# Second MLP's third token tile by seven block products of 256 columns, some collects by accumulating DMA, and weight rings divided by part

## The chip, the core and the metric

The kernel runs on one NeuronCore of a Trainium2 chip. Five engines run their own instruction streams beside each other: TensorE (PE in the profile) multiplies matrices, VectorE (DVE), ScalarE (ACT) and GpSimd (POOL) work on elements, SyncE (SP) issues DMAs. They wait for one another by semaphores. The metric is the time of one execution on the device in microseconds (us), the median of several.

## The reference

Attention with decay over blocks of 64 positions gives x, 1,536 tokens by 512. Two MLPs follow:

```python
x = np.ascontiguousarray(attn_out.transpose(0, 2, 1, 3)).reshape(B * S, H * D)   # 1536 x 512
h = x @ w_in                      # first MLP, 512 x 2048
g = h * np.clip(h + 3.0, 0.0, 6.0) / 6.0
x = g @ w_out                     # 2048 x 512
h = x @ w_in                      # second MLP, other weights
g = np.maximum(0.01 * h, h)
out = g @ w_out
```

The weights come as 64-bit numbers and are turned into fp32 in the kernel. Every fp32 operand of an MLP is split into a high and a low part (names ending in `h` and `l`), and a product is three matmuls: high x high, high x low, low x high.

## The kernel before, in words

The tokens are three tiles `t` of 512 columns, the 2,048 hidden units 16 slices `f` of 128. For a slice, `gemm1` makes the hidden 128 x 512 values of a tile: four chunks of the 512 inputs by three matmuls, 12 matmuls. A gate on ScalarE and VectorE makes `Gh` and `Gl` of them, and `gemm2` adds the slice's part to four banks `acc0` to `acc3` in PSUM, three matmuls each. Slices go in blocks (`BLOCKS`): after a block's last slice `collect` moves the four banks of a tile away and adds them to the tile's sums in SBUF (`SUM[t]`); ScalarE copies them in a first block, VectorE adds them in later ones, and in the first MLP's last two blocks banks 0 and 2 are instead filled with the sums before the block begins (`seeded`).

Tiles 0 and 1 (`PAIR`) are not multiplied so from the first MLP's fourth block on: two slices and two tiles form a 2 x 2 block product, made with seven products of 6 matmuls instead of eight (`pair`, `product`). S1 to S4 are sums of weight blocks, T1 to T4 sums of x blocks, `keep` copies a partial result and `join` adds two. The third tile goes on with `gemm1` (`one`).

The order on every engine comes from a planner, `Order`: operations are added with an engine, a planned cost, what they follow, which buffers they take and free, and a due time; `issue` plays the plan and writes the instructions in the order in which they start there. The due times of the paired blocks come from the list `line`. A weight half goes through `load_w` (DMA on SP into a `raw` buffer), `low_bits`, `magnitude`, `exponent`, `compose`, then `w_high` (ScalarE) and `w_low` (VectorE). Before, a slice's two halves, w_in (`j = 0`) and w_out (`j = 1`), lie in one buffer of the ring `w`, taken and freed together.

Of the kernel before, what the change touches and what calls it, by code (L numbers as in the profile page):

```python
# [20 lines left out]
DM = H * D  # L21
# [95 lines left out]
def decay_attention_two_mlps(ctx: ExitStack, tc: tile.TileContext, qkk, vv, lam, w1, w2, out):  # L117
# [3 lines left out]
    sizes = {"raw": 4, "cv": 3, "cl": 2, "w": 6, "G": 3, "u": 3, "h": 2, "a": 2, "r": 3, "vs": 3}  # L121
# [246 lines left out]
    cut = lambda l, f, j, hl: W[l, f][hl][:, j, :]  # L368
# [38 lines left out]
    def w_high(h):  # L407
        def fn(_):
            l, f, j = h
            if j == 0:  # L410
                W[l, f] = [new("w", [P, 2, DM], F32R, n) for n in ("wh", "wl")]
            nc.scalar.copy(out=cut(*h, 0), in_=CV[h][0].bitcast(F32))  # L412
        return fn

    def w_low(h):
        return lambda e: eng[e].tensor_tensor(out=cut(*h, 1), in0=CV[h][0].bitcast(F32), in1=cut(*h, 0).bitcast(F32),  # L416
                                              op=ALU.subtract)
# [24 lines left out]
    alloc_w, composed, low = {}, {}, {}  # L442
    for l in range(2):
        for f in range(NF):
            for j in range(2):
# [8 lines left out]
                hi = add(("act", 0.62), w_high(h), after=[c, alloc_w.get((l, f))], takes=[] if j else ["w"])  # L454
                alloc_w[l, f] = hi
# [10 lines left out]
    PH, U, G, ACC = {}, {}, {}, {}  # L466

    def gemm1(s):
        def fn(_):
            l, b, t, f = steps[s]  # L470
            xh, xl = X[t]
            wh, wl = W[l, f]
            ps = PH[s] = new("a" if paired(l, f) else "h", [P, TT], F32)
            n = 0
            for k in range(KC):
                ws = slice(k * P, (k + 1) * P)
                for a, x in ((wh, xh), (wh, xl), (wl, xh)):
                    nc.tensor.matmul(ps, a[:, 0, ws], x[:, k, :], start=(n == 0), stop=(n == 3 * KC - 1))  # L478
                    n += 1
# [34 lines left out]
    seeded = lambda s, e: steps[s][0] == 0 and steps[s][1] >= SINGLE and e % 2 == 0  # L514
# [8 lines left out]
    def gemm2(s, e):  # L523
        def fn(_):
            l, b, t, f = steps[s]
            wh, wl = W[l, f]
# [8 lines left out]
            if l == 0:  # L535
                terms = ((wh[:, 1, es], gh), (wh[:, 1, es], gl), (wl[:, 1, es], gh))
            else:
                terms = ((gh[:, es], wh[:, 1]), (gh[:, es], wl[:, 1]), (gl[:, es], wh[:, 1]))
# [3 lines left out]
            PA["acc", s, e] = ACC[e]  # L542
        return fn

    def collect(s, e):
        def fn(x):
            l, b, t, f = steps[s]
            ps, acc = PA["acc", s, e], SUM[t][:, e, :]
            if b and not seeded(s, e):
# [3 lines left out]
        return fn  # L553

    def split_x(t, e, lo):
        def fn(_):
            xh, xl = (x[:, e:e + 2] for x in X[t])
            if lo:
                nc.vector.tensor_tensor(out=xl, in0=SUM[t][:, e:e + 2], in1=xh.bitcast(F32), op=ALU.subtract)
            else:  # L560
                nc.scalar.copy(out=xh, in_=SUM[t][:, e:e + 2])
        return fn
# [11 lines left out]
    PAIR = (0, 1)  # L574
    XT, CS, SPARE = {}, {}, {}
    A_B = (("A11", "B11"), ("S1", "T1"), ("A12", "B21"), ("S2", "T2"), ("S4", "B22"), ("S3", "T3"), ("A22", "T4"))
    BANK = (0, 2, 1, 0, 2, 0, 0)

    def open_late(_):
# [4 lines left out]
        for n in ("T1", "T2", "T4"):  # L584
            XT[n] = [xt.tile([P, 2, TT], F32R, name=f"{n}{i}") for i in "hl"]
        (XT["B11"], XT["B21"]), (XT["T3"], XT["B22"]) = (
            [[x[:, e:e + 2] for x in X[t]] for e in (0, 2)] for t in PAIR)

    def whole(n):
        t, e = {"B11": (0, 0), "T1": (0, 0), "B21": (0, 2), "T4": (0, 2),  # L590
                "B12": (1, 0), "T3": (1, 0), "B22": (1, 2), "T2": (1, 2)}[n]
        return SUM[PAIR[t]][:, e:e + 2]

    def x_sum(n, a, b):
        return lambda _: nc.vector.tensor_tensor(out=whole(n), in0=whole(a), in1=whole(b), op=ALU.subtract)

    def x_split(n, lo, src=whole):
        def fn(e):
            xh, xl = XT[n]
            if lo:  # L600
                eng[e].tensor_tensor(out=xl, in0=src(n), in1=xh.bitcast(F32), op=ALU.subtract)
            else:
                nc.scalar.copy(out=xh, in_=src(n))
        return fn


    def spare(n):
        i = {"B11": 0, "T1": 0, "B12": 1, "T3": 1, "B22": 2, "T2": 2, "B21": 3, "T4": 3}[n]
        return SPARE[i // 2][:, i % 2]

    def x_whole(n):
        t, e = {"B11": (0, 0), "B21": (0, 2), "B12": (1, 0), "B22": (1, 2)}[n]

        def fn(g):
            if n in ("B11", "B22"):
                SPARE[n == "B22"] = pool["s"].tile([P, 2, 2, TT], F32, tag="s", name="x_spare")
            xh, xl = (x[:, e:e + 2].bitcast(F32) for x in X[PAIR[t]])
            eng[g].tensor_tensor(out=spare(n), in0=xh, in1=xl, op=ALU.add)
        return fn

    def x_diff(n, a, b):
        return lambda e: eng[e].tensor_tensor(out=spare(n), in0=spare(a), in1=spare(b), op=ALU.subtract)

    def product(l, p, i):
        def fn(_):
            an, bn = A_B[i]
            if i < 2:
                PA["S", l, p, BANK[i]] = new("h", [P, TT], F32)
            ps, xs = PA["S", l, p, BANK[i]], XT[bn]
            if an[0] == "S":  # L630
                ws = [SB[l, p][:, hl, int(an[1]) - 1] for hl in range(2)]
# [253 lines left out]
```

## Time and profile before

| what | value |
|---|---|
| median of 3 runs (567.62 to 570.68) | 568.48 us |
| the profiled execution's own time | 570.67 us |
| its span, first to last instruction | 568.5 us |
| busy share PE, DVE, ACT, POOL | 98%, 76%, 58%, 5% |
| mean granted clock of TensorE | 0.991 |

An engine's busy share says how long it had an instruction, not that it was the limit: what an engine waited for, and the chain of work that ended last, tell that.

### The profile page before, as it was taken

What the parts mean: (1) busy time and instruction counts of PE and PEld (TensorE: products, weight loads), DVE (VectorE), ACT (ScalarE), POOL (GpSimd) and SP (SyncE); (2) the same over time, 40 slices, a digit from 0 to 9 for tenths busy, and PEclk for the clock granted to TensorE, in tenths of its full rate; (3) what the DMA queues carried; (4) which work ended last, traced back from release to release, by engine and by line L of the source; (5) the groups of instructions that cost most, each with busy time, mean ns of one, the idle gap of its engine ahead of it and who ended that gap; (6) DMA issues with size and microseconds to landing.
All of it is one profiled execution on the core that took longest, in us unless ns stands there. A gap on an engine that the chain in (4) does not pass through costs nothing.

```text
span 568.5 us, 8504 instructions
## 1 busy us (share of the span) xinstructions
PE 554.9 (98%) x3372; PEld 460.3 (81%) x3372; DVE 430.0 (76%) x696; ACT 329.1 (58%) x554; POOL 28.2 (5%) x33
## 2 busy tenths in 40 slices
PE   8879999999999999999999999999999999999996
PEld 5778888888888888888888888888888888888885
DVE  8668999998998988789798896778754988552222
ACT  5677885555355775488575885687336744343110
POOL 6543000000000000000000000000000000000000
PEclk9798999999999999999999999999999999999999
DMA  8884233331023202221220222422211121000332
GB/s 336 313 320 148 81 108 108 112 112 39 0 75 110 76 37 75 79 107 37 76 74 1 74 75 74 149 74 75 79 70 37 39 77 35 0 1 0 75 74 74
DMA packets 14536, 49.81 MB, mean 88 GB/s; under 512 B 1698, under 2 KB 1698, under 8 KB 14498
## 3 DMA queue, kind: packets, MB, share of 16 engines
q1 hardware_dynamic: 14176, 48.77, 25.6%
q8 instruction: 26, 0.43, 0.3%
q10 hardware_dynamic: 322, 0.52, 0.3%
q14 instruction: 12, 0.10, 0.1%
HBM read 46.14 MB, written 3.15 MB: 87 GB/s over the span
## 4 chain that ended last, share of the span: by engine, by line
PE 96%; issue 1%; DMA 1%; POOL 1%; DVE 0%; SPq 0%; POOLq 0%
PE acc L540 44%; PE h L638 17%; PE h L478 12%; PE a L478 11%; PE a L638 3%; PE pair L274 2%; PE a L299 2%; PE h L311 2%; PE a L540 2%; DMA vs<-vv 1%; DVE sums L550 0%; POOL kd L264 0%; PE h L179 0%; POOL vs L260 0%; SPq L243 0%
## 5 line engine op out<-in xcount | busy, mean ns | idle before, releaser
L550 DVE TENSOR_TENSOR sums<-acc,sums 128x512 f32<-128x512 f32 x68 | 45.6, 688 | 24.8 <-PE acc L540 24.8
L507 DVE TENSOR_TENSOR Gl<-u,Gh 128x512 fp32r<-128x512 f32 x32 | 22.1, 689 | 45.2 <-ACT Gh L658 45.2
L540 PE MATMUL acc<-Gh,wh 128*128 128x512 f32 x144 | 56.1, 390 | 0.0
L540 PE MATMUL acc<-Gh,wl 128*128 128x512 f32 x144 | 56.0, 389 | 0.0
L540 PE MATMUL acc<-Gl,wh 128*128 128x512 f32 x144 | 56.0, 389 | 0.0
L540 PE MATMUL acc<-wh,Gh 128*128 128x512 f32 x128 | 49.8, 389 | 0.0
L540 PE MATMUL acc<-wl,Gh 128*128 128x512 f32 x128 | 49.8, 389 | 0.0
L540 PE MATMUL acc<-wh,Gl 128*128 128x512 f32 x128 | 49.8, 389 | 0.0
L664 ACT ACTIVATE u<-a 128x512 f32<-128x512 f32 x24 | 14.4, 599 | 59.4 <-PE a L478 57.6
L416 DVE TENSOR_TENSOR wl<-t,wh 128x512 fp32r<-128x512 f32 x64 | 43.0, 686 | 7.4 <-ACT wh L412 7.3
L404 DVE CUSTOM_DVE_ANT_0 t<-t,c 128x1024 uint16<-128x1024 uint16 x64 | 45.2, 706 | 2.2
L412 ACT CAST wh<-t 128x512 fp32r<-128x512 f32 x64 | 39.1, 617 | 13.0 <-DVE t L404 12.1
L381 ACT ACTIVATE c<-raw 128x512 uint32<-128x512 uint32 x64 | 42.8, 671 | 4.8 <-DVE t L404 3.6
L385 ACT ACTIVATE t<-raw 128x512 f32<-128x512 f32 x64 | 42.7, 666 | 4.6 <-DVE wl L416 4.6
L402 DVE SCALAR_TENSOR_TENSOR t<-raw,t 128x512 uint32<-128x512 uint32 x64 | 44.1, 689 | 1.3
L487 ACT ACTIVATE u<-h,three 128x512 f32<-128x512 f32 x28 | 19.3, 689 | 40.6 <-PE h L478 36.9
L478 PE MATMUL h<-xh,wh 128*128 128x512 f32 x96 | 37.6, 391 | 0.0
L478 PE MATMUL h<-xh,wl 128*128 128x512 f32 x96 | 37.4, 389 | 0.0
L478 PE MATMUL h<-xl,wh 128*128 128x512 f32 x96 | 37.4, 389 | 0.0
L478 PE MATMUL a<-xh,wh 128*128 128x512 f32 x96 | 37.3, 389 | 0.0
L478 PE MATMUL a<-xl,wh 128*128 128x512 f32 x96 | 37.3, 389 | 0.0
L478 PE MATMUL a<-xh,wl 128*128 128x512 f32 x96 | 37.3, 389 | 0.0
(149 smaller groups left out, 1315.9 us busy)
## 6 DMA issues: line engine op xcount, KB each, us to landing
raw<-w SPq DMA_DIRECT2D x64, 512.0 KB, 3.3
sums<-qkk SPq DMA_DIRECT2D x12, 768.0 KB, 7.2
vs<-vv SPq DMA_DIRECT2D x6, 512.0 KB, 7.1
out<-sums SPq DMA_DIRECT2D x20, 128.0 KB, 2.4
out<-sums ACTq DMA_DIRECT2D x4, 128.0 KB, 3.2
lam_sb<-lam ACTq DMA_DIRECT2D x1, 0.0 KB
```

Of the source, the lines that this page charges most:

```text
L381: nc.scalar.activation(out=CV[h][1], in_=RAW[h][:, :, 0], func=AF.Copy, scale=2.0 ** -29)
L385: return lambda _: nc.scalar.activation(out=CV[h][0].bitcast(F32), in_=RAW[h][:, :, 1].bitcast(F32), func=AF.Abs)
L402: nc.vector.scalar_tensor_tensor(out=t, in0=RAW[h][:, :, 1], scalar=0xC0000000, in1=t, op0=ALU.bitwise_and, op1=ALU.bitwise_or)
L404: nc.vector.tensor_tensor(out=t, in0=t, in1=c, op=ALU.add)
L412: nc.scalar.copy(out=cut(*h, 0), in_=CV[h][0].bitcast(F32))
L416: return lambda e: eng[e].tensor_tensor(out=cut(*h, 1), in0=CV[h][0].bitcast(F32), in1=cut(*h, 0).bitcast(F32), op=ALU.subtract)
L478: nc.tensor.matmul(ps, a[:, 0, ws], x[:, k, :], start=(n == 0), stop=(n == 3 * KC - 1))
L487: nc.scalar.activation(out=U[s], in_=at_src(s), func=AF.Relu, bias=three, scale=1.0)
L507: nc.vector.tensor_tensor(out=gl, in0=U[s], in1=gh.bitcast(F32), op=ALU.subtract)
L540: nc.tensor.matmul(ACC[e], a, x, start=(first and n == 0 and not seeded(s, e)), stop=(last and n == 2), skip_group_check=seeded(s, e))
L550: nc.vector.tensor_tensor(out=acc, in0=ps, in1=acc, op=ALU.add)
L638: nc.tensor.matmul(ps, ws[a][:, k * P:(k + 1) * P], xs[b][:, k], start=(i < 2 and n == 0), stop=(n == 5), skip_group_check=True)
```

## The change

The third tile of the second MLP is cut into two halves of 256 columns, and they are multiplied with two slices by the same seven products, each of 256 columns (`half_pair`, `product_1`, `keep_1`, `join_1`); `gemm1` stays for the first MLP. The seven products are put into another order. In every block but a first and a last one of each MLP, banks 0 to 2 are collected in another way: ScalarE copies the bank into a buffer of the new ring `st`, and GpSimd issues a DMA that adds it to the sums in SBUF (`by_dma`, `add_up`). In the first MLP's last block all four banks are seeded, and the second tile's sums of that block are read from PSUM directly (`sums_pair`, `late_x`). The sums of x blocks for the first MLP are begun by DMAs (`x_whole`) where VectorE made them. The ring `w` becomes `w0` and `w1`, each of half slices, and `raw` has 3 buffers where it had 4.

The diff, cut to its core:

```diff
-    sizes = {"raw": 4, "cv": 3, "cl": 2, "w": 6, "G": 3, "u": 3, "h": 2, "a": 2, "r": 3, "vs": 3}
+    sizes = {"raw": 3, "cv": 3, "cl": 2, "w0": 4, "w1": 5, "st": 2, "G": 3, "u": 3, "h": 2, "a": 2, "r": 3, "vs": 3}
...
-            l, f, j = h
-            if j == 0:
-                W[l, f] = [new("w", [P, 2, DM], F32R, n) for n in ("wh", "wl")]
-            nc.scalar.copy(out=cut(*h, 0), in_=CV[h][0].bitcast(F32))
+            W[h] = [new(f"w{h[2]}", [P, DM], F32R, n) for n in ("wh", "wl")]
+            nc.scalar.copy(out=W[h][0][:, cols(*h)], in_=CV[h][0].bitcast(F32)[:, cols(*h)])
...
-                hi = add(("act", 0.62), w_high(h), after=[c, alloc_w.get((l, f))], takes=[] if j else ["w"])
-                alloc_w[l, f] = hi
+                hi = add(("act", 0.62), w_high(h), after=[c], takes=[f"w{j}"])
...
-    seeded = lambda s, e: steps[s][0] == 0 and steps[s][1] >= SINGLE and e % 2 == 0
+    seeded = lambda s, e: steps[s][0] == 0 and steps[s][1] == len(BLOCKS[0]) - 1
+    by_dma = lambda s, e: e < 3 and 0 < steps[s][1] < len(BLOCKS[steps[s][0]]) - 1
+    kept = lambda s, e: seeded(s, e) and steps[s][2] == PAIR[1]
+    STAGE, ACC_AT = {}, {}
+
+    def add_up(s, e):
+        t = steps[s][2]
+        return lambda _: nc.gpsimd.dma_start(out=SUM[t][:, e, :], in_=STAGE[t, e], accum_op=ALU.add)
...
+            if by_dma(s, e):
+                STAGE[t, e] = new("st", [P, TT], F32)
+                nc.scalar.copy(out=STAGE[t, e], in_=ps)
+            elif b and not seeded(s, e):
                 nc.vector.tensor_tensor(out=acc, in0=ps, in1=acc, op=ALU.add)
...
-    A_B = (("A11", "B11"), ("S1", "T1"), ("A12", "B21"), ("S2", "T2"), ("S4", "B22"), ("S3", "T3"), ("A22", "T4"))
-    BANK = (0, 2, 1, 0, 2, 0, 0)
+    A_B = (("A11", "B11"), ("S1", "T1"), ("S2", "T2"), ("A12", "B21"), ("S3", "T3"), ("S4", "B22"), ("A22", "T4"))
+    BANK = (0, 2, 0, 1, 0, 2, 0)
...
+    def x_whole(k, n, lo):
+        def fn(_):
+            if not lo and (n == "B11" or n == "B22" and not k):
+                SPARE[k, int(n == "B22")] = pool["s"].tile([P, 2 << k, 2, TT >> k], F32, tag="s", name=f"x_spare{k}")
+            x = part([x[lo].bitcast(F32) for x in X], k, n)
+            if lo:
+                nc.gpsimd.dma_start(out=spare(k, n), in_=x, accum_op=ALU.add)
+            else:
+                nc.sync.dma_start(out=spare(k, n), in_=x)
+        return fn
...
+    def product_1(l, p, i):
+        def fn(_):
+            if i == 0:
+                PA["X", l, p] = new("a", [P, TT], F32)
+            terms(l, p, i, 1, PA["XY"[i in (2, 4, 6)], l, p][:, hi_cols if i in (1, 5) else lo_cols], i == 0)
+        return fn
+
+    def keep_1(l, p, i):
+        def fn(_):
+            x = PA["X", l, p]
+            if i:
+                CS[l, p, "5"] = new("ux", [P, TT], F32)
+                nc.scalar.copy(out=CS[l, p, "5"][:, lo_cols], in_=x[:, hi_cols])
             else:
-                k = 2 * P * (int(an[2]) - 1)
-                ws = [w[:, 0, k:k + 2 * P] for w in W[l, 2 * p + int(an[1]) - 1]]
-            n = 0
-            for k in range(2):
-                for a, b in ((0, 0), (0, 1), (1, 0)):
-                    nc.tensor.matmul(ps, ws[a][:, k * P:(k + 1) * P], xs[b][:, k], start=(i < 2 and n == 0),
-                                     stop=(n == 5), skip_group_check=True)
-                    n += 1
-        return fn
+                PA["Y", l, p] = new("a", [P, TT], F32)
+                nc.scalar.copy(out=PA["Y", l, p][:, lo_cols], in_=x[:, lo_cols])
+        return fn
+
+    def join_1(l, p, n):
+        return lambda _: nc.vector.tensor_tensor(out=PA[n, l, p][:, hi_cols], in0=PA["Y", l, p][:, lo_cols],
+                                                 in1=CS[l, p, "5"][:, lo_cols], op=ALU.add)
...
+            far = by_dma(s, e)
+            c = add(("dve", 0.69) if b and not in_seed and not far else ("act", 0.58), collect(s, e),
+                    due2[s] + T_COLLECT, after=[prev2, *([] if far else taken.get((t, e), []))], frees=[bank],
+                    takes=["st"] * far)
+            bank_last[bank] = c
+            if far:
+                c = add(("pool", 1.2), add_up(s, e), due2[s] + T_COLLECT, after=[c, *taken.get((t, e), [])])
+                c = add(("dma2", 2.5), nothing, due2[s] + T_COLLECT, after=[c], frees=["st"])
...
+        if l:
+            line = [*(two(0, i) for i in range(4)), one(0), *(two(1, i) for i in range(4)), one(2), two(2, 0), two(2, 1)]
...
+    def half_pair(l, p, after_a):
+        f1, f2 = 2 * p, 2 * p + 1
+        d, at = due_p["1", l, f1], 0
+        ops = []
+
+        def prod(i, after=(), takes=()):
+            nonlocal at
+            an, bn = A_B[i]
+            w = s_ready[l, p] if an[0] == "S" else w_ready[l, 2 * p + int(an[1]) - 1, 0]
+            ops.append(add(("pe", 0.72), product_1(l, p, i), d + at, after=[w, *x_op[l, 1, bn], *ops[-1:], *after],
+                           takes=list(takes)))
+            last_s[l, 1, bn] = ops[-1]
+            at += 0.72
+            return ops[-1]
+
+        k1 = add(("act", 0.42), keep_1(l, p, 0), after=[prod(0, after_a, takes=["a", "a"])])
+        k5 = add(("act", 0.42), keep_1(l, p, 1), after=[prod(1)], takes=["ux"])
+        v = add(("dve", 0.42), join_1(l, p, "X"), after=[prod(2, [k1]), k5])
+        p2 = prod(3)
+        c22 = add(("dve", 0.42), join_1(l, p, "Y"), after=[prod(4, [v])], frees=["ux"])
+        p3 = prod(5, [v])
+        p4 = prod(6, [c22])
+        for f, n, after in ((f1, "X", [p2, p3]), (f2, "Y", [p4, c22])):
+            s = at_step[l, 2, f]
+            add_ps = add(("none", 0.0), lambda _, s=s, n=n: PH.__setitem__(s, PA[n, l, p]), after=after)
+            gates(s, [add_ps], "a")
+        half_at[0] = ops[0]
+        return ops
...
+        ops = [pair(l, f // 2) for f in fs[::2]]
+        for f, o in zip(fs[::2], ops):
+            if l:
+                add(("none", 0.0), nothing, after=o + half_pair(l, f // 2, ops[1][3:4]), frees=["s", "w0", "w0"])
```

How the built programs stand. TensorE, second MLP, third block, third tile: before, the hidden values of one slice (`x` 105 and 106 are the tile's high and low part, `a` the PSUM bank), first rows of 12 with the group ahead:

```order
L540 MATMUL acc_4403<-wl,Gh 128x512
L540 MATMUL acc_4403<-wh,Gl 128x512
L478 MATMUL a<-xh_105,wh 128x512
L478 MATMUL a<-xl_106,wh 128x512
L478 MATMUL a<-xh_105,wl 128x512
```

And after, second block, third to fifth product of a pair of slices (T21 is T2 for the half tiles, `s` a sum of weight blocks, `acc` 4298 and 4323 banks 0 and 1, in brackets the engines whose semaphores are waited for):

```order
L546 MATMUL acc_4298<-wh,Gl 128x512 [waits DVE_49]
L636 MATMUL a<-T21h,s 128x256 [waits Activation_49]
L636 MATMUL a<-T21l,s 128x256
L636 MATMUL a<-T21h,s 128x256 x2
L636 MATMUL a<-T21l,s 128x256
L636 MATMUL a<-T21h,s 128x256
L636 MATMUL a<-xh_111,wh 128x256 [waits Activation_49]
L636 MATMUL a<-xl_112,wh 128x256
L546 MATMUL acc_4323<-wh,Gh 128x512
L636 MATMUL a<-xh_111,s 128x256 [waits DVE_49]
```

What moved: two slices' 24 matmuls of 512 columns stood in two closed pieces that waited for nothing of their own; now 42 of 256 columns stand between groups of `gemm2`, and the third, fourth, fifth and seventh product wait for copies and joins of earlier ones.

ScalarE after, at the end of the second block's first tile of the second MLP (`acc0` to `acc2` are its banks; `a` and `ux` the half products' PSUM bank and buffer):

```order
L557 COPY st_4118<-acc0_4000 128x512 [waits PE_49]
L557 COPY st_4125<-acc1_4016 128x512 [waits PE_49]
L664 COPY a_4148<-a_4137 128x256 [waits PE_49]
L557 COPY st_4156<-acc2_4024 128x512 [waits DMASW7_49,Activation_49]
L661 COPY ux_4164<-a_4137 128x256 [waits PE_49]
L686 ACTIVATE Gxh_4182<-ux_4004 128x512 [waits DVE_49,PE_49]
```

At the same place before, the collects stood on VectorE:

```order
L550 TENSOR_TENSOR sums_100<-acc0_3886,sums_100 128x512 [waits PE_49]
L550 TENSOR_TENSOR sums_100<-acc1_3906,sums_100 128x512 [waits PE_49]
L550 TENSOR_TENSOR sums_100<-acc2_3912,sums_100 128x512 [waits PE_49]
L550 TENSOR_TENSOR sums_100<-acc3_3920,sums_100 128x512 [waits PE_49]
```

What moved: three of four collects went from VectorE to ScalarE, and the copy of bank 2 has a wait for a DMA that GpSimd issued, with the copy of the second half product (`ux`) behind it.

## Rows read from the trace of the kernel before

**Rows 1.** The page: span, busy time of each engine, granted clock in 40 slices.

```profile
span 568.5 us, 8504 instructions
PE 554.9 (98%) x3372; PEld 460.3 (81%) x3372; DVE 430.0 (76%) x696; ACT 329.1 (58%) x554; POOL 28.2 (5%) x33
...
PEclk9798999999999999999999999999999999999999
```

**Rows 2.** The waits of PE: us in total, times, longest.

```profile
PE pair L274 <- issue: 5.5, 2, 3.2
PE a L299 <- POOL kd L264: 1.1, 1, 1.1
PE h L179 <- DVE zeros L184: 1.1, 1, 1.1
PE a L299 <- issue: 0.7, 1, 0.7
PE h L311 <- POOL vs L260: 0.2, 1, 0.2
```

**Rows 3.** The chain that ended last: start us, us, what.

```profile
37.79 3.20 issue
...
472.32 2.72 PE a L478 x12
...
548.48 5.44 PE acc L540 x24
556.64 4.77 PE acc L540 x21
561.43 2.73 DVE sums L550 x4
```

**Rows 4.** Busy us by stretch; after POOL come granted clock, DMA share, GB/s.

```profile
312.00:370.00 58.00, 58.00 (x257) 47.86 (x257) 45.82 (x79) 42.53 (x73) 0.00 (x0) 1.00 0.27 91
...
430.00:490.00 60.00, 60.00 (x266) 49.71 (x265) 46.15 (x78) 32.05 (x55) 0.00 (x0) 1.00 0.14 45
```

**Rows 5.** Timeline of matmuls (PE) and weight loads (PEld): start us, us.

```profile
400.30 0.39 PE L540 MATMUL acc<-wl,Gh 128*128 128x512 f32 x1
400.31 0.19 PEld L540 LDWEIGHTS acc<-wh,Gl 128*128 128x128 f32 x1
400.53 0.39 PE L540 MATMUL acc<-wh,Gl 128*128 128x512 f32 x1
```

**Rows 6.** Weight loads by form: count, busy us, mean ns, idle before.

```profile
L478 PEld LDWEIGHTS a<-xh,wh 128*128 128x128 f32 x96 | 18.0, 188 | 3.8
...
L274 PEld LDWEIGHTS pair<-sums 64*64 64x64 f32 x384 | 13.7, 145 | 7.3 <-issue 5.7 <-DMA sums<-qkk 0.4 <-ACT vs L304 0.4
L179 PEld LDWEIGHTS <-zeros 128*128 128x128 bf16 x18 | 1.7, 115 | 3.2 <-issue 1.4 <-DVE zeros L184 1.1
```

**Rows 7.** Timeline of PE in the warm-up and the attention.

```profile
12.32 1.04 PE L179 MATMUL h<-zeros 128*128 128x512 bf16 x4
...
31.20 1.15 PE L274 MATMUL pair<-sums 64*64 64x64 f32 x32
32.27 1.15 PE L299 MATMUL a<-vs,kd 128*64 128x64 f32 x32
```

**Rows 8.** Groups on ACT and DVE: count, busy us, mean ns, idle before.

```profile
L552 ACT COPY sums<-acc 128x512 f32<-128x512 f32 x34 | 19.8, 589 | 4.3 <-PE acc L540 2.8
L664 ACT ACTIVATE u<-a 128x512 f32<-128x512 f32 x24 | 14.4, 599 | 59.4 <-PE a L478 57.6 <-PE a L638 1.8
L213 ACT COPY u<-h 128x252 f32<-128x252 f32 x1 | 0.4, 369 | 0.9 <-PE h L208 0.9
...
L550 DVE TENSOR_TENSOR sums<-acc,sums 128x512 f32<-128x512 f32 x68 | 45.6, 688 | 24.8 <-PE acc L540 24.8
L507 DVE TENSOR_TENSOR Gl<-u,Gh 128x512 fp32r<-128x512 f32 x32 | 22.1, 689 | 45.2 <-ACT Gh L658 45.2
L428 DVE TENSOR_TENSOR raw<-t 128x256 f32<-128x256 f32 x24 | 10.1, 420 | 0.2
L404 DVE CUSTOM_DVE_ANT_0 t<-t,c 128x1024 uint16<-128x1024 uint16 x64 | 45.2, 706 | 2.2
```

**Rows 9.** DMA issues (KB each, median us to landing), and POOL's longest group.

```profile
raw<-w SPq DMA_DIRECT2D x64, 512.0 KB, 3.3
sums<-qkk SPq DMA_DIRECT2D x12, 768.0 KB, 7.2
...
out<-sums SPq DMA_DIRECT2D x20, 128.0 KB, 2.4
...
L264 POOL TENSOR_TENSOR kd<-sums,decay 64x512 f32<-64x512 f32 x22 | 25.2, 1145 | 18.4 <-issue 9.3 <-PE a L299 5.8 <-POOL kd L264 2.4
```

More of the change, by code (lines that the diff above doesn't have):

```diff
@@ L594, in x_sum @@
[L594 to L599, printed above, removed]
+        for k in range(2):
+            for n in ("T1", "T2", "T4"):
+                XT[k, n] = [xt.tile([P, 2, TT >> k], F32R, name=f"{n}{k}{i}") for i in "hl"]
+            for n in ("B11", "B21", "T3", "B22"):
+                XT[k, n] = [part([x[i] for x in X], k, n) for i in range(2)]
@@ L604, in x_split @@
         return fn
[L607 to L618, printed above, removed]
-        return fn
@@ new lines, in terms @@
+    def terms(l, p, i, k, ps, first):
+        an, bn = A_B[i]
+        xs = XT[k, bn]
+        if an[0] == "S":
+            ws = [SB[l, p][:, hl, int(an[1]) - 1] for hl in range(2)]
+        else:
+            c = 2 * P * (int(an[2]) - 1)
+            ws = [w[:, c:c + 2 * P] for w in W[l, 2 * p + int(an[1]) - 1, 0]]
+        n = 0
+        for c in range(2):
+            for a, b in ((0, 0), (0, 1), (1, 0)):
+                nc.tensor.matmul(ps, ws[a][:, c * P:(c + 1) * P], xs[b][:, c], start=(first and n == 0),
+                                 stop=(n == 5), skip_group_check=True)
+                n += 1
@@ L685, in second @@
                 continue
-            c = add(("dve", 0.69) if b and not in_seed else ("act", 0.58), collect(s, e), due2[s] + T_COLLECT,
-                    after=[prev2, *taken.get((t, e), [])], frees=[bank])
+            if kept(s, e):
+                sums.append(prev2)
+                continue
+            far = by_dma(s, e)
[6 more added lines that the diff above has]
+                c = add(("dma2", 2.5), nothing, due2[s] + T_COLLECT, after=[c], frees=["st"])
             sums.append(c)
-            bank_last[bank] = c
             taken[t, e] = [c]
@@ L708, in decay_attention_two_mlps @@
             due_p[item] = at
-            at += 9.52 if item[0] == "S" else 2.72
-        rest = [] if end else [two(2, 2), two(2, 3)]
+            at += {"S": 9.52, "1": 5.04 if l else 2.72, "2": 2.72}[item[0]]
+        rest = [two(2, i) for i in range(3 if end else 2, 4)]
     for item in rest:
@@ L772, in pair @@
             gate[s] = add(("dve", 0.69), g_low(s), after=[gh], frees=[free]), n
-        add(("none", 0.0), nothing, after=ops, frees=["s"])
+        return ops
     def seconds(l, b):
@@ L785, in decay_attention_two_mlps @@
             if steps[s][1] == b:
[L786 removed]
+                g = one(s, x_of(steps[s][2]))
+                calm = g if steps[s][2:] == (1, starts[0][2] - 1) else calm
         seconds(0, b)
     op_late = add(("none", 0.0), open_late, after=att_ops, frees=[n for n in late for _ in range(late[n])])
[L792 to L796 removed]
```

245 lines of the change are left out of this document (143 added, 102 removed).

## The prediction

> **What bounds the kernel now.** The first view is the page's busy table: TensorE (PE) is busy for 98% of the span of 568.5 us, VectorE for 76%, ScalarE for 58% [rows 1]. A share alone proves nothing, so the second view is what TensorE waited for: five rows, 8.6 us in all, and every one of them belongs to the attention or the warm-up at the start [rows 2]. After the attention TensorE waits for nobody. The third view is the chain that ended last: its last pieces are TensorE, TensorE, TensorE and then four collects on VectorE, 561.43 to 564.16 us, with the store behind them [rows 3]. In the second MLP the stretches say the same: TensorE is busy for all of 312 to 370 us and of 430 to 490 us, at granted clock 1.00, which is its level of 2.4 GHz, while VectorE is busy for 45.8 of 58.0 us and 46.2 of 60.0 us, and ScalarE for 42.5 and 32.1 us [rows 4]. So from some 70 us on time is saved only by fewer TensorE microseconds, and lost by anything that makes TensorE wait. Relief for VectorE is worth nothing by itself.
>
> **TensorE's work.** Before, the third token tile of the second MLP takes 12 matmuls of 512 columns for each slice f, 16 slices, 192 matmuls. The chain has twelve of them as one piece of 2.72 us [rows 3], so one takes 2.72/12 = 0.2267 us (the 0.39 us of one record is with its latency; the next one starts 0.23 us later [rows 5]). Removed: 192 x 0.2267 = 43.5 us. Added: for each of 8 pairs of slices 7 products of 6 matmuls of 256 columns, 336 matmuls. The trace has no such matmul, so its pace must be bounded.
>
> Streaming 512 columns at 2.4 GHz is 0.2133 us, so 0.0133 us of the pace is a fixed part or grows with the columns. If it grows, 256 columns take 0.1133 us, and 336 take 38.1 us: 5.4 us gained. If it is fixed, they take 0.1067 + 0.0133 = 0.120 us, 40.3 us in all: 3.2 us gained. From above: each matmul brings its own weights, and a load of 128 columns has a record of 0.188 us, which starts 0.01 us after the matmul before it [rows 5, 6]. If a load could start only when the one before it had ended, the pace would be 0.188 us, 63.2 us in all: 19.6 us lost. The break-even is 43.5/336 = 0.1295 us. Which end is nearer? In the attention, 32 records of 64 columns, each with its own load of 64 columns, go from 31.20 to 32.27 us, 0.033 us each, though one such load has a record of 0.145 us [rows 6, 7]. Loads therefore overlap, and the record of a load is mostly latency. A load of 64 columns each 0.033 us is 0.067 us for 128, or 0.134 us if two loads on different halves of the array ran at once there. And the warm-up's bf16 matmuls of 512 columns, with loads of 0.115 us, go at (1.04 - 0.39)/3 = 0.217 us [rows 6, 7], only 0.010 us faster: a part for each matmul that depends on the kind of load and hardly on the columns. I take 0.120 us.
>
> One place of the Trainium skill (TensorE: Matmul & The Clock Gate, Measured speedup vs the span model) says that a weight load overlaps running matmuls only where its row group differs. These loads use all 128 rows and still run beside the matmul before them [rows 5], so the trace disagrees. By that rule load and stream would follow each other, and the time would be that of the second rival's far end.
>
> **What TensorE may wait for.** Three chains are new; each is followed here through the order of after, with durations from rows.
>
> First, the half-width products among themselves. The third product waits for a copy of the first one's result, the fourth for a copy of the second one's, the fifth and seventh for joins on VectorE. Between the second product's end and the fourth's start TensorE has one product and one group of three, 0.72 + 0.68 = 1.40 us; the copy takes 0.37 us (a ScalarE copy of 252 columns [rows 8]), and a join 0.42 us (VectorE on 256 columns). So there is 1.0 us for one other ScalarE operation of 0.6 to 0.7 us ahead of it. Cost: nothing; without that cover 0.4 us a pair, 3.2 us in all.
>
> Second, the gates of the last two slices. The last one waits for the seventh product; then two ScalarE operations of 0.60 us and one on VectorE of 0.69 us follow [rows 8], about 2.1 us with the end of the matmul, and TensorE has the four groups of the slice before, 2.72 us. Nothing.
>
> Third, the collects by DMA: 45 of them (five blocks, three tiles, three banks). Each replaces a VectorE addition of 0.688 us by a ScalarE copy of 0.589 us into `st`, a DMA that POOL issues, and an accumulation in memory [rows 8]. `st` has two buffers, so the copy of bank 2 waits until bank 0's sum has landed, and the first group of the next tile on bank 2 waits for that copy. The narrowest place is the end of the first tile in blocks 1 and 2 of the second MLP: TensorE has, from bank 0's last matmul to bank 2's next group, five groups of three (3.40 us) and three half products (2.16 us), 5.56 us. The end of the matmul (0.16 us beyond its pace), two copies of 0.59 us and hand-overs of 0.03 us each leave about 4.1 us for the DMA from issue to landing. The next narrowest are four tile ends in the first MLP, with 6.1 us and so about 4.7 us; all others have 7.0 us or more. Behind the waiting copy on ScalarE stands the copy of the second half product, and TensorE's fourth product waits for that in turn, so the whole lateness shows on TensorE. Nothing in the trace issues a DMA from POOL or accumulates in one. By the nearest rows 128 KB land in 2.4 us and 512 KB in 3.3 us when the queues are quiet [rows 9], so 256 KB plain are 2.7 us. From above I add, for reading both addends, the price of 512 KB, and, for POOL's work, one POOL operation of 1.15 us [rows 9]: 4.45 us. Under load the worst row is 7.2 us. I take 3.6 us, in the middle of 2.7 and 4.45: no wait, or 0.35 us at two places if it is the upper value. I put 0.2 us into the sum.
>
> The Trainium skill (SBUF — State Buffer, SBUF: two separate sides) warns that VectorE's two-port modes lock GpSimd out while it writes descriptors. No run here shows it yet. The operation that it could speak of, the 1,024-element one of the weight decoding, lasts 0.71 us [rows 8], so by that rule a landing would come up to 0.7 us later: 5.2 us at the upper value, which is the third rival below.
>
> **What costs nothing.** VectorE loses 31.0 us of additions (45 x 0.688) and gains 16 joins of 0.42 us, 7 us, and about as much of splits and differences of the third tile; ScalarE gains about 41 copies of 0.59 us net, 24 us over 430 us. At 58% it has room. The weight rings shrink from six whole slices to four and five halves. The narrowest reuse is that of a w0 half: freed by the last half product of one pair, needed one block on after some 17 us of TensorE work, against about 6 us of casts and sums. The x sums of the first MLP leave VectorE for DMAs and are needed more than 60 us of TensorE work after their start. The seeds of the first MLP's last block put eight ScalarE copies of 0.59 us behind one another; the second bank may be late there by 0.1 us, once. Head and tail have the same operations.
>
> **The sum.** -43.5 + 40.3 + 0.2 = -3.0 us. The profiled execution took 570.67 us, 2.17 us beyond its span, so its like would take 567.7 us; it lies 2.19 us above the median of 568.48 us, and on the median's scale the sum is 565.5 us.
>
> **The rivals.**
> 1. Forecast: 565.5 us, with 564.3 to 566.5 us for the small terms and the measurement. Chance 0.54.
> 2. The load is not hidden behind 256 columns. Place: the 336 half-width matmuls. For it: the record of 0.188 us; against it: loads that follow each other at 0.033 us. It decides from a pace of 0.1295 us on; at 0.134 us the kernel loses 1.5 us (570.2 us with the waits), at 0.188 us it takes 588 us. Chance 0.13.
> 3. The accumulated sums land late. Place: bank 2's first group after a tile end. From 4.1 us on two places wait, from 4.7 us on six; at 5.0 us that is 2 x 0.9 + 4 x 0.3 = 3.0 us, and the gain is gone (568.3 us); at 5.3 us the kernel is at 570 us. For it: no row of such a DMA, and additions queued on POOL one behind the other; against it: quiet queues after 70 us. Chance 0.20.
> 4. The fixed part is not fixed: 0.1133 us, 5.4 us gained, 563.3 us. Chance 0.13.
>
> That the change does not do what it says is excluded: the order of after has the 336 matmuls.
>
> 0.5% of the median is 2.8 us, about what a measurement here can tell from no change. Faster by more (below 565.6 us): rival 4 and a little over half of the forecast, 0.45. Same: the rest of the forecast, most of rival 3 and a little of rival 2, 0.39. Slower: the upper parts of rivals 2 and 3, 0.16. The range leaves out the far parts of rivals 2 and 3 and a margin below rival 4: 562.8 to 569.5 us.
>
> **What the profile after will show.** Right: half-width matmuls 0.120 us apart, 2,040 other matmuls of the MLPs at 0.2267 us, no row of TensorE waiting for ScalarE at a tile end, last matmul 3 us earlier, some 3.5 to 4 us between issue and landing of a sum. Wrong: a pace above 0.130 us; a wait of TensorE for a copy into `st` or of ScalarE for a DMA; or a head that moves, since one fetch stall of 3.20 us stands in the chain there [rows 3] and the weight loads that share the queues with it have changed their ring.

## The result and the profile after

The changed kernel takes 576.11 us (median of 4 runs, 574.59 to 577.12), the kernel before 569.37 us beside it (567.62 to 570.68): ratio 1.0135, interval 1.0105 to 1.0165. It is 1.4% slower, where 0.5% faster was forecast (565.5 us), and lies outside the range of 562.8 to 569.5 us. The profiled execution took 576.62 us, with a span of 574.8 us.

The page of the kernel after, which answers to [rows 1]:

```profile
span 574.8 us, 9014 instructions
...
PE 554.1 (96%) x3516; PEld 462.1 (80%) x3516; DVE 403.7 (70%) x675; ACT 352.8 (61%) x617; POOL 72.0 (13%) x82
...
q0 software_dynamic: 7056, 13.90, 13.8%
```

TensorE is busy for less time than before, and its share has fallen: it waits. Its waits, and two waits of other engines (engine, line, waited for: us in total, times, longest):

```profile
PE acc L546 <- ACT st L557: 6.7, 3, 4.2
...
ACT st L557 <- DMA sums<-st: 19.6, 7, 5.5
...
DVE x_spare L603 <- DMA x_spare<-xl: 3.8, 1, 3.8
```

The first row is the one that the prediction named as the sign of its third rival; beside [rows 2], it is the only one of TensorE's waits that doesn't belong to the head. The starts of TensorE's matmuls show three gaps: 1.89 us after 94.85 us, 4.33 us after 115.92 us and 0.95 us after 233.27 us. All three lie in the first MLP, and none in the second. The chain of the stretch from 90 to 126 us shows what each link waits for:

```profile
90.08 6.15 DMA sums<-st
...
96.33 0.59 ACT st L557
...
100.47 6.78 DMA x_spare<-xh
107.25 0.34 issue
107.59 0.85 POOL x_spare L620
108.45 11.38 DMA sums<-st
...
119.85 0.59 ACT st L557
120.44 0.04 issue
120.48 5.74 PE acc L546 x18
```

One sum takes 6.15 us to land and another 11.38 us, where the median is the 3.7 us of the second row (the list of DMA issues, to be read beside [rows 9]); the quickest of the 45 took 3.2 us:

```profile
raw<-w SPq DMA_DIRECT2D x64, 512.0 KB, 3.3
sums<-st POOLq DMA_DIRECT2D x45, 256.0 KB, 3.7
...
x_spare<-xh SPq DMA_DIRECT2D x4, 512.0 KB, 7.1
x_spare<-xl POOLq DMA_DIRECT2D x4, 512.0 KB, 7.2
```

What stood in front of them is seen in the queues' packets. Two sums are issued one behind the other from 90.08 us on. Up to 93.7 us only q1, the queue of the weight loads, moves anything; then q0, the queue of the accumulating transfers, fills the engines (packets, MB, share of 16 engines; the stretches 90.2 to 93.7 and 93.7 to 96.2 us):

```profile
q1 hardware_dynamic: 104, 0.43, 58.0%
...
q0 software_dynamic: 241, 0.46, 100.9%
q1 hardware_dynamic: 40, 0.10, 10.1%
```

The first packet of a sum (of the first one, where two are issued together) comes 1.42 to 1.54 us after the issue where the load queue is empty or nearly done, and 2.2 to 3.7 us after it in the four cases where a load of 512 KB was under way until then. The sum issued at 108.45 us stood behind x transfers of 512 KB on its own queue besides.

The wait of 4.33 us costs more than its length, as the stretches of TensorE behind it show (sums of busy time and records; after POOL come granted clock, DMA share and GB/s):

```profile
116.00:120.00 4.00, 0.31 (x2) 0.00 (x0) 1.99 (x3) 0.15 (x1) 0.87 (x1) 1.00 1.08 267
120.40:123.20 2.80, 2.71 (x6) 2.15 (x7) 1.89 (x3) 1.82 (x5) 1.75 (x2) 0.50 1.01 189
123.20:126.00 2.80, 2.80 (x13) 2.32 (x12) 2.29 (x4) 2.10 (x4) 0.00 (x0) 0.97 1.04 194
```

After four almost idle microseconds the granted clock is 0.50, which is the level of 1.2 GHz, and matmuls start 0.43 us apart instead of 0.2267 us: some 1.5 us more. After the waits of 1.89 and 0.95 us it stayed at 2.4 GHz.

The account from the first matmul of the first MLP to the last of all: 511.50 us before (51.55 to 563.05 us), 519.21 us after (49.92 to 569.13 us), 7.7 us longer. Waits give 1.89 + 4.33 + 0.95 = 7.2 us, the lower clock 1.5 us, small gaps around them 0.6 us, and the half products take 1.6 us back, as a later run shows. The head is 1.6 us shorter in this execution; over the runs of this study the start of the first MLP varies from 47.3 to 51.6 us.

The half products do run at the pace taken, 0.12 us apart, but not at every place (matmuls and weight loads from the end of a pair's fourth product to its sixth, with the groups of `gemm2` between them: start us, us, and idle time before it with its releaser):

```profile
370.08 0.28 PE L636 MATMUL a<-xl,wh 128*128 128x256 f32 x1
370.20 0.28 PE L636 MATMUL a<-xh,wl 128*128 128x256 f32 x1
370.21 0.19 PEld L546 LDWEIGHTS acc<-wh,Gh 128*128 128x128 f32 x1
...
370.79 0.40 PE L546 MATMUL acc<-wh,Gl 128*128 128x512 f32 x1
...
371.08 0.19 PEld L636 LDWEIGHTS a<-xh,s 128*128 128x128 f32 x1 [0.33 <-DVE a L668]
371.08 0.39 PE L636 MATMUL a<-xh,s 128*128 128x256 f32 x1
...
371.30 0.28 PE L636 MATMUL a<-xl,s 128*128 128x256 f32 x1
...
371.90 0.40 PE L546 MATMUL acc<-wh,Gh 128*128 128x512 f32 x1
372.13 0.40 PE L546 MATMUL acc<-wl,Gh 128*128 128x512 f32 x1
372.37 0.39 PE L546 MATMUL acc<-wh,Gl 128*128 128x512 f32 x1
372.60 0.28 PE L636 MATMUL a<-xh,s 128*128 128x256 f32 x1
```

Elsewhere a weight load starts beside the matmul ahead of it. Here, at the fifth product (371.08 us), it had to wait for VectorE's join; so the matmul starts 0.06 us late, and the next one 0.10 us. TensorE's waits above don't list such places; the waits of its weight loads (PEld) do, for joins (L668) and for copies (L664):

```profile
PEld a L636 <- DVE a L668: 1.7, 5, 0.3
PEld a L636 <- ACT a L664: 1.4, 7, 0.2
```

From the first half product (341.05 us) to the last matmul, TensorE takes 1.6 us more than 0.120 and 0.2267 us for each matmul. By the starts in the timeline this has three parts. Eight places at which a weight load waited for a copy or a join lose 0.07 to 0.17 us each, 1.1 us in all. The matmuls of 512 columns that follow a half product lose 0.9 us: at all 47 such places the first two of them take 0.233 and 0.236 us on average until the next one starts (the last rows above), and the kernel before has no such place. What slows them no run shows. The other half-width matmuls go 0.119 us apart, which gives 0.4 us back.

### The profile page after: what moved, and what is told of

Read it like the earlier page. It is cut to its first block, busy times and chain, and to the rows that moved or that the text cites. A ratio compares the mean times of both kernels' runs of the same rounds, so it can differ in the third digit from the quotient of the medians.

```text
span 574.8 us, 9014 instructions
## 1 busy us (share of the span) xinstructions
PE 554.1 (96%) x3516; PEld 462.1 (80%) x3516; DVE 403.7 (70%) x675; ACT 352.8 (61%) x617; POOL 72.0 (13%) x82
## 4 chain that ended last, share of the span: by engine, by line
PE 72%; issue 12%; DMA 5%; POOL 1%; ACT 1%; DVE 0%; SPq 0%; POOLq 0%; ACTq 0%
PE acc L546 36%; PE h L636 14%; PE a L636 10%; PE h L476 8%; DMA sums<-st 4%; PE a L476 2%; POOL sums L519 1%; DMA x_spare<-xh 1%; PE a L546 1%; PE h L311 1%; ACT st L557 1%; PE a L299 1%; PE pair L274 0%; ACT u L485 0%; DVE sums L559 0%
## 5 line engine op out<-in xcount | busy, mean ns | idle before, releaser
L519 POOL DMA_DIRECT2D sums<-st x45 | 39.7, 939 | 417.6 <-ACT st L557 397.4
L410 ACT CAST wh<-t 128x512 fp32r<-128x512 f32 (+1 forms) x64 | 37.7, 594 | 15.5 <-PE h L476 9.9
L414 DVE TENSOR_TENSOR wl<-t,wh 128x512 fp32r<-128x512 f32 (+1 forms) x64 | 41.4, 652 | 7.0 <-ACT wh L410 6.9
L557 ACT COPY st<-acc 128x512 f32<-128x512 f32 x41 | 24.0, 588 | 31.7 <-DMA sums<-st 19.6
L391 DVE TENSOR_SCALAR t<-t 128x512 f32<-128x512 f32 x64 | 26.9, 421 | 20.5 <-ACT t L385 20.4
L546 PEld LDWEIGHTS acc<-Gh,wh 128*128 128x128 f32 x144 | 27.4, 190 | 12.9 <-ACT st L557 7.2
```

What stands on the lines that cost most here:

```text
L391: nc.vector.tensor_scalar(out=t.bitcast(F32), in0=t.bitcast(F32), scalar1=MAG_MIN, scalar2=MAG_MAX, op0=ALU.max, op1=ALU.min)
L410: nc.scalar.copy(out=W[h][0][:, cols(*h)], in_=CV[h][0].bitcast(F32)[:, cols(*h)])
L414: return lambda e: eng[e].tensor_tensor(out=W[h][1][:, cols(*h)], in0=CV[h][0].bitcast(F32)[:, cols(*h)], in1=W[h][0].bitcast(F32)[:, cols ...
L519: return lambda _: nc.gpsimd.dma_start(out=SUM[t][:, e, :], in_=STAGE[t, e], accum_op=ALU.add)
L546: nc.tensor.matmul(ACC[e], a, x, start=(first and n == 0 and not seeded(s, e)), stop=(last and n == 2), skip_group_check=seeded(s, e))
L557: nc.scalar.copy(out=STAGE[t, e], in_=ps)
```

## The experiments

The theory after this result: accumulated sums that land late hold ScalarE's copies into `st`, and these hold TensorE; weight loads and x transfers on the same DMA engines make them late. The rivals: the divided weight rings, VectorE's load, and half products that give nothing. Each run is compared with the kernel before on its own chip (medians 567.5 to 568.2 us).

**Block sums or x sums?** Four runs take the accumulating transfers back to VectorE, in parts.

```diff
  # first run (fourth run: True in place of the condition)
-            if by_dma(s, e):
+            if by_dma(s, e) and steps[s][0] == 0:
+                nc.vector.tensor_tensor(out=acc, in0=ps, in1=acc, op=ALU.add)
+            elif by_dma(s, e):
  # second run; the third has both edits
-                nc.gpsimd.dma_start(out=spare(k, n), in_=x, accum_op=ALU.add)
-            else:
-                nc.sync.dma_start(out=spare(k, n), in_=x)
+                nc.vector.tensor_tensor(out=spare(k, n), in0=hi, in1=x, op=ALU.add)
```

First run: 

> The first MLP's block sums are added by VectorE straight from PSUM, at the places where the changed kernel's plan has ScalarE's copies; the x sums still go by DMA, the second MLP's sums too. Theory (accumulating transfers that land late hold ScalarE's copies, and these hold TensorE): the waits of 1.89, 4.33 and 0.95 us and the some 1.5 us at half clock behind the second go, so 576.1 - 8.7 = 567.4 us, and no accumulator in the first MLP waits over 0.5 us. Rival A (weight rings: w comes late, the sums only show it): the waits come back at the same places behind w, 573 to 576 us. Rival B (VectorE can't carry the added 27 sums of 0.69 us in the first MLP): waits for VectorE's sums, over 570 us.

Measured: 573.59 us, ratio 1.0100 (1.0072 to 1.0128). The first and third waits went, the large one came back under another name (the waits of 90 to 125 us):

```profile
PE acc L548 <- DVE sums L558: 4.7, 1, 4.7
...
DVE x_spare L607 <- DMA x_spare<-xl: 3.9, 1, 3.9
```

So the theory as expected here fell by half. VectorE reaches its first difference of x sums at 112.9 us, waits 3.90 us for the x transfer, and the block's third sum stands behind it in VectorE's order. The x transfers reach TensorE by this way too.

Second run: 

> The four x sums are added by VectorE as in the kernel before; all block sums by DMA as in the changed kernel. Theory (two causes of lateness: weight loads in flight, and the x transfers ahead in the ring): the wait of 4.33 us near 116 us goes or falls under 2 us, with the half clock behind it; those of 1.89 and 0.95 us stay, so about 576.1 - 5.5 = 570.6 us. Rival A (only weight loads matter): the wait near 116 us stays at 2 us or more, about 574 us. Rival B (x transfers cause all of it, through shifted weight loads): all three go, 567.4 us.

Measured: 569.88 us, ratio 1.0041 (1.0022 to 1.0060): under the changed kernel by 6.2 us of the medians, or 0.94% of the ratios, 5.3 us. The gap near 116 us and the lower clock are gone; gaps of 1.71 and 1.47 us stay:

```profile
PE acc L546 <- ACT st L557: 2.9, 2, 1.6
```

This is what the theory gave. Some two thirds of the loss came with the x transfers.

Third run: 

> Both: the first MLP moves no sum by DMA at all, the second MLP's block sums still do. Theory: as the first of these runs, 567.4 us, since x transfers without late block sums cost TensorE nothing. Rival A (the x transfers also delay weight loads): 0.5 us or more below the first run. Rival B (VectorE has no room for both): waits for VectorE, over 569 us.

Measured: 569.47 us, ratio 1.0033 (1.0012 to 1.0054). No wait for a DMA, but two gaps of 0.96 and 1.03 us behind VectorE's sums, in a stretch where VectorE runs without a pause and carries, beside the x sums, block sums that the plan had put on ScalarE. That is rival B: taking all of it back in the same order removes one wait and makes another.

Fourth run: 

> All block sums of both MLPs are added by VectorE; only the x sums go by DMA. Theory (in the second MLP sums by DMA neither cost nor give TensorE anything): the same as the first run, 567.4 us, within 0.5. Rival: VectorE's 18 added sums of the second MLP come late for gates there, over 568.5 us.

Measured: 574.32 us, ratio 1.0111 (1.0066 to 1.0155), within what can be told from the first run, with the same gap near 113 us (3.74 us). In the second MLP the sums by DMA cost nothing in the changed order, and the relief for VectorE gave nothing: from the first half product to the last matmul TensorE takes 228.09 us in the first run, with these sums by DMA, and 228.08 us in this one, without.

**The ring.** The fifth and sixth run keep the x sums on VectorE and leave the ring of two less to hold, or make it longer.

```diff
  # fifth run: two sums of a tile by DMA in the first MLP, replanned
-    by_dma = lambda s, e: e < 3 and 0 < steps[s][1] < ...
+    by_dma = lambda s, e: e in ((0, 1) if steps[s][0] == 0 else (0, 1, 2)) and 0 < steps[s][1] < ...
  # sixth run, in its place
-    "w1": 5, "st": 2
+    "w1": 4, "st": 4
```

Fifth run: 

> The x sums by VectorE, and in the first MLP only the sums of the first two output chunks of a tile by DMA (the third by VectorE, planned so); half products and second MLP as changed. Theory (ScalarE's third copy waits for the first one's landing because the ring has two buffers): with two copies per tile no copy waits, the stalls of 1.71 and 1.47 us of the second run go, 569.9 - 3.2 = 566.7 us. Rival A (VectorE is full there, as in the third run, whose sums came 0.96 and 1.03 us late): waits for VectorE's sums of 1 us or more, 568 us or over. Rival B (w is what comes late): stalls behind w, 569 us or over.

Measured: 566.79 us, ratio 0.9972 (0.9950 to 0.9993). No gap of TensorE over 0.25 us after the head. Landings were not faster (3.3 us at least, 3.8 at the median, 7.5 at most), only hardly anybody waits for them; of the 12.1 us that ScalarE waited for landings in the second run this is left, and TensorE has no such row:

```profile
ACT st L557 <- DMA sums<-st: 1.2, 2, 0.6
```

Sixth run: 

> The x sums by VectorE; four staging buffers for sums in place of two, and, to make room, four pairs of buffers in place of five for the second weights. All three sums of a tile by DMA. Theory: landings stay as late as in the second run (first packets up to 3.8 us after the issue), but no copy waits for them, so TensorE's stalls of 1.71 and 1.47 us go: 566.7 us. Rival A (late transfers delay weight loads as well, and these hold TensorE): stalls of about the same size behind weights, 569 us or over. Rival B (the weight ring was needed at five): new waits for wl or wh, over 568 us.

Measured: 567.52 us, ratio 0.9992 (0.9971 to 1.0013). ScalarE waits for no landing, though these are the slowest of all at the median (4.8 us, 7.7 at most); both stalls are gone, and one of 1.29 us before a block product at 196.6 us is new, behind VectorE:

```profile
PE h L635 <- DVE u L489: 1.1, 1, 1.1
```

Both runs say that the ring of two was the link. The new wait isn't one for weights, though its stretch holds VectorE's work on weights; whether the shorter weight ring or the new plan put it there is open. These two runs, and the later ones that change the plan, have all engines ordered anew by the planner, so more moves than the lines shown; that the ring was the link rests on the waits for landings, which went from 12.1 us in the second run to 1.2 us and to none.

**The half products.** The seventh and twelfth run undo them alone, with `one()` in place of `half_pair()`, the line of due times of the kernel before, and the split of the third tile's x without differences. The seventh keeps three sums by DMA in the second MLP, the twelfth two.

```diff
-                add(("none", 0.0), nothing, after=o + half_pair(l, f // 2, ops[1][3:4]), frees=["s", "w0", "w0"])
+                add(("none", 0.0), nothing, after=o, frees=["s"])
+                for i in (f, f + 1):
+                    g = one(at_step[l, 2, i], [split[0], split[2], *ops[1][3:4]])
+                    half_at[0] = half_at[0] if i % 2 else g
+                    add(("none", 0.0), nothing, after=[*o, g], frees=["w0"])
```

Seventh run: 

> As the fifth run (x sums by VectorE, two sums by DMA in the first MLP), but the second MLP's third tile by twelve matmuls of 512 columns per step, in the order of the kernel before, without half products. Theory (336 matmuls at 0.120 us in place of 192 at 0.2267 us give 3.2 us, and about 1 us goes to the places where 256 and 512 columns meet): 2.1 us over the fifth run, 568.8 us. Rival A (the half products give nothing at the end of the kernel): within 0.5 us of the fifth run. Rival B (the places where widths meet cost nothing in all): 3.2 us over it.

Measured: 576.16 us, ratio 1.0140 (1.0110 to 1.0170), 9.4 us over the fifth run, which no theory had. In the order of before the ring of two stalls TensorE in the second MLP, for 3.22 us near 425 us and 2.19 us near 492 us, the first with the lower clock behind it (the windows of 420 to 428 and 428 to 432 us):

```profile
420.00:428.00 8.00, 5.13 (x23) 3.92 (x21) 2.92 (x5) 1.38 (x3) 1.77 (x2) 1.00 0.80 198
428.00:432.00 4.00, 3.81 (x10) 3.00 (x11) 2.60 (x5) 3.12 (x7) 0.87 (x1) 0.57 0.39 68
```

ScalarE's waits have the cause:

```profile
ACT st L557 <- DMA sums<-st: 16.4, 5, 5.2
```

Twelfth run: 

> As the seventh run (third tile of the second MLP by matmuls of 512 columns), but in the second MLP too only two sums of a tile go by DMA. Theory (the seventh run's extra time was the ring of two, whose stalls of 3.22 and 2.19 us and half clock stood in the second MLP; the half products' own worth is what is left): no stall over 1 us, and 1.6 us over the fifth run, that is 568.4 us. Rival A (half products are worth the full 3.2 us of their columns): 570.0 us. Rival B (they are worth nothing): 566.8 us. Rival C (the order of the kernel before stalls here whatever the ring): over 572 us.

Measured: 568.35 us, ratio 1.0014 (0.9995 to 1.0033); no gap over 0.25 us. It is 1.56 us over the fifth run by the medians, which come from two chips (by the ratios to the kernel before 2.4 us, each known to 0.2%). The account within one execution is sharper: from the first matmul of the first MLP to the last its TensorE takes 511.43 us, against 509.89 us in the fifth run, 509.88 us in the tenth below and 511.50 us before. The half products are worth 1.55 us, half of what their columns alone would give. That the twelfth run has one sum less by DMA per tile doesn't enter, since no gap for a sum is left in either.

**What the late sums wait for.** The eighth run issues each weight load as two of 256 KB; else it is the second run.

```diff
+            for n in (slice(0, DM), slice(DM, 2 * DM)):
-                nc.sync.dma_start(out=RAW[h]..., in_=(w1, w2)[l][f, j].bitcast(U32))
+                nc.sync.dma_start(out=RAW[h]...[:, n], in_=(w1, w2)[l][f, j].bitcast(U32)[:, n])
```

> As the second run (x sums by VectorE, all three sums by DMA, ring of two), but every weight load is issued as two of 256 KB each, one behind the other. Theory (a transfer of the sums waits until the load queue has run empty): first packets stay up to 2.7 to 3.8 us after the issue where loads are under way, the stalls of 1.71 and 1.47 us stay, 569.9 us. Rival (it waits only for the transfer then in flight): the delays shrink to about 1.3 us over the usual 1.43 us, the stalls fall under 0.7 us each, 568 us.

Measured: 568.77 us, ratio 1.0020 (0.9995 to 1.0045). The latest landing falls from 8.5 to 6.4 us and the first packet of the sum near 88 us comes after 2.52 instead of 3.79 us, one half of a load earlier; but others still take 2.5 to 2.7 us, the gaps are 0.74, 1.12 and a new 0.72 us, and the times of the two runs overlap. It leans to the rival, by which a sum waits for the one transfer in flight, and doesn't settle it.

**The x transfers alone.** Ninth run: two sums by DMA as in the fifth, x sums by DMA as changed. The tenth adds one line, which puts VectorE's differences of x sums later in the plan; the eleventh has that line in the changed kernel.

```diff
             w[n] = add(("pool", 3.5), x_whole(k, n, 1), after=[last])
+            w[n] = add(("none", 8.0), nothing, after=[w[n]])
```

Ninth run: 

> As the fifth run (two sums by DMA in the first MLP, the third by VectorE), but the x sums by DMA as in the changed kernel. Theory (the x transfers cost by two ways, sums behind them in the ring and VectorE's first difference of x sums waiting for their landing with a tile's sums behind it): the first way is closed here, the second is open, so a stall of 4 to 5 us near 115 us with some 1.5 us at half clock: 566.8 + 5.9 = 572.7 us. Rival (they cost only by way of the staging ring): no stall over 1 us there, 566.8 us.

Measured: 573.41 us, ratio 1.0101 (1.0074 to 1.0128). VectorE waits 5.0 us for the x transfer; this time a gate stands behind it in VectorE's order, and TensorE waits for that, at 115 us for 3.14 us and then at the lower clock:

```profile
DVE x_spare L603 <- DMA x_spare<-xl: 5.0, 1, 5.0
...
PE acc L546 <- ACT Gh L495: 3.0, 1, 3.0
```

Tenth run: 

> As the ninth run, but the plan gives each x transfer 8 us more to land, which puts VectorE's first difference of x sums some 33 places later in its order. Theory: nothing waits for the x transfers any more, no stall over 1 us, 566.8 us like the fifth run, and VectorE does four additions of 1.22 us less than there. Rival A (the x transfers delay weight loads, which then hold TensorE): stalls behind w, over 568 us. Rival B (the later x sums hold the first product blocks): a stall before the first block product, over 568 us.

Measured: 566.11 us, ratio 0.9970 (0.9950 to 0.9989). The x transfers take as long as in the ninth run (8.6 us at the median for the accumulating ones), and from 62 us to the first half products no gap of TensorE exceeds 0.1 us. This and the fifth run are faster than both kernels, by 0.3% against the kernel before.

Eleventh run: 

> The changed kernel (three sums by DMA, ring of two) with VectorE's differences of x sums put later as in the tenth run and nothing else. Theory (with all three sums by DMA the ring alone holds TensorE): the stall near 116 us stays at 3 us or more behind ScalarE's copy, with the half clock behind it, and so do those of 1.9 and 0.95 us: 575 to 576.5 us. Rival (VectorE's wait was the cause in the changed kernel as well): the stall near 116 us goes, about 570.3 us.

Measured: 579.26 us, ratio 1.0200 (1.0172 to 1.0229); slower than the theory's 575 to 576.5 us, by one more stall of 2.31 us near 158 us and a longer stretch at the lower clock (119.7 to 125.4 us, granted clock 0.50). All four hang on the ring:

```profile
ACT st L557 <- DMA sums<-st: 20.1, 5, 6.3
...
PE acc L546 <- ACT st L557: 8.5, 4, 4.2
```

Put together, in us (medians from three chips and the result's own, on which the kernel before took 567.5 to 569.4 us):

| block sums of a tile by DMA in the first MLP | x by DMA | x by DMA, differences later | x by VectorE |
|---|---|---|---|
| three | 576.11 | 579.26 | 569.88 |
| two | 573.41 | 566.11 | 566.79 |
| none | 573.59 | not run | 569.47 |

Two waits stood at the same tile end, ScalarE's for `st` and VectorE's for the x transfer. Closing only the one (two by DMA, or none) or only the other (differences later) leaves the stall near 115 us; closing both, or taking the x transfers away, ends it.

## Why the prediction was wrong

**The step that failed** is the term of 0.2 us for waits in the sum, and with it the weight of the third rival (0.20). In its place the runs showed 7.2 us of waits, 1.5 us at the lower clock behind the longest of them and 0.6 us of small gaps. Two statements of the prediction led there: "quiet queues after 70 us", and that the x sums go to DMAs that cost nothing. The mechanism of that rival, its place (bank 2's first group after a tile end) and its sign in the profile were all as written. The median landing came to 3.7 us where 3.6 us was taken; that was the middle between two bounds, so its closeness says little for the working. And a median doesn't decide at a place where one late transfer shows in full. From issue to landing sums took up to 11.4 us, beyond the 7.2 us that stood as the worst row under load and had no part in the choice of 3.6 us. The queues were not quiet: the rows of before have the DMA engines busy for 0.27 of 312 to 370 us [rows 4], and in the four cases where a weight load of 512 KB kept the engines until then a sum's first packet came 2.2 to 3.7 us after the issue.

**The narrowest places** were counted as TensorE's work between two points, with one landing time for all: second MLP first, four tile ends of the first MLP next. In the changed order the second MLP never waited: the landings that its tile ends hang on, those of bank 0's sums, took 3.3 to 3.7 us. Two of the three stalls came at first-MLP tile ends where the count left 4.7 us; the sums there took 6.15 us (issued at 90.08 us) and 5.14 us (at 228.57 us). The longest stall came at an end that the count held to be wide: TensorE had 8.8 us of work there, from 107.3 to 116.1 us, which by the prediction's own allowances leaves some 7.4 us, and the sum behind the x transfers took 11.38 us.

**The x sums** were costed by when their results are needed, 60 us later. That VectorE's first difference stands in a strict order, with a block's sum or a gate behind it, was left out: every wait of that operation is a wait of what stands behind it (first, ninth and tenth run). This and the queueing of sums behind the x transfers cost 5 to 6 us together (second run).

**The half products** gain by the mechanism forecast, at 0.119 to 0.120 us, but 1.55 us, not 3.2 us. The term was mis-sized by 1.6 us in two ways. The cover of 1.40 us for copies and joins, taken to cost nothing, is too short at eight places, where the weight load can't run ahead: 1.1 us. And the matmuls of 512 columns between the half products were taken at 0.2267 us, where those that follow one are slower: 0.9 us, its cause open (0.4 us came back by the pace of 0.119 us). The seventh run's expectation had put about 1 us on the places where widths meet. The second and the fourth rival fell. The Trainium skill's rule that weight loads overlap running matmuls only in another row group (TensorE: Matmul & The Clock Gate, The mechanism) is not borne out here: the loads use all 128 rows, last 0.19 us and run beside the matmul ahead of them. That rule would have cost more than the far end that the prediction gave it: load and stream one behind the other are 0.188 + 0.107 = 0.29 us, an estimate from the prediction's figures.

**Held:** the weight rings (no wait of TensorE for wh or wl in any of these runs), ScalarE's room, the gates of the last slices, and that relief for VectorE by itself is worth nothing in the second MLP. The ring `raw` of three buffers, which has a say in when loads start, was not tried by itself. The lock between VectorE's modes and POOL's descriptors (the Trainium skill, SBUF — State Buffer, SBUF: two separate sides) isn't seen beside the 1,024-element operation: the sum issued at 266.75 us, with one running from 267.18 us, had its first packet after 1.43 us, as sums without it had. Beside a TENSOR_SCALAR of 128 x 512 on VectorE the sum issued at 214.06 us took 1.52 us, and one at 204.77 us in the eighth run 1.69 us, so 0.1 to 0.25 us may come from such an operation; no run tests that.

## What to carry to other kernels

Cost a transfer that others wait for by its landing behind the largest transfer that can stand before it, at the place of the wait, not by its median; if the two straddle the slack, lengthen the ring or send fewer through it. An operation that waits for a transfer on an engine with a strict order makes everything behind it wait: put it late in the order, as one planned delay of 8 us did here, worth 7 us (ninth to tenth run). And what seems free because its result is needed late isn't free if its consumer stands early.

## What was not expected of the hardware

A transfer of sums issued while a weight load was in flight moved no packet until that load's packets were all but through, even when both could begin at the same time: of the sum issued at 90.08 us the first packet came at 93.8 us, where the load's first came at 91.5 us (the two stretches above). The Trainium skill (DMA: Bandwidth & Descriptors, Queues, rings and completion order) has each DMA engine take turns between its queues and drain a whole packet, typically 9 to 17 descriptors, before it changes. The eighth run agrees in part: with half the load in front, one delay fell by 1.27 us, others less or not at all (2.70 to 2.52 us, 3.16 to 2.70 us, 1.95 to 2.07 us).

A 4.33 us stall of TensorE cost some 1.5 us more at 1.2 GHz, and one of 4.40 us in the eleventh run some 2.8 us, while stalls of 1.89, 2.19 and 2.31 us cost only themselves. A product whose first weight load waits for another engine loses 0.07 to 0.17 us even when TensorE shows no wait. And the first two matmuls of 512 columns behind one of 256 lose 7 and 9 ns, with no wait on record.
